# An attention and mixture-of-depths kernel: 1/rms rows stored ahead of the k and v loads, broadcast half a section later, six warm-up products, and tasks moved

## The chip, the cores and the metric

The kernel runs on one core of a Trainium2 chip. Its time is the device time of one execution in microseconds; lower is better. The core's engines are TensorE (PE, the matmuls), VectorE (DVE), ScalarE (ACT), GpSimd (POOL) and SyncE (SP); 16 DMA engines move data between memory and the core. Each engine executes its own list of instructions strictly in order and waits at an instruction until what it depends on is done. SP does no arithmetic here: it issues almost all of the DMAs, in the order of its list.

## What is computed

Per batch of 8: attention of 12 heads over 448 tokens with head size 64, q and k divided by their root mean square, and then a mixture of depths on the 768-wide result: the 128 tokens of each batch with the highest gate score go through a two-layer network.

```python
# q, k, v: (8, 12, 448, 64)
rms = np.sqrt(np.mean(x * x, axis=-1, keepdims=True) + 1e-06)   # of q and of k
q_n, k_n = q / rms_q * g_q, k / rms_k * g_k
scores = q_n @ k_n.T / sqrt(64)
attn = softmax(scores)
x = attn @ v                                  # -> (8, 448, 768)
score = x @ w_gate                            # (8, 448)
top = 128 tokens with the highest score, per batch
out = x.copy()
out[top] = x[top] + sigmoid(score[top]) * (relu(x[top] @ w1) @ w2)   # w1: 768 x 1024
```

Everything is float32.

## The kernel before, in words

**Groups and sections.** Four heads of one batch are a group n, so there are 24 groups. A group has 7 units of 64 keys; for each unit `scores` multiplies k by q (L395), ACT takes the exponential (L404), `values` multiplies by v (L419), and `add_probs` sums the exponentials over the units on DVE (L435). The main loop goes through sections q = 0 to 23, one per group. In section q PE does the scores and values of group q, and between them the finishing work of group q - 1: `sum_keys` (L462, the sums over keys), `invert_sums` (L485, L487) and two transposes back to tokens, `to_tokens` (L517 on PE, L519 on DVE, which evacuates). The first 8 sections (`FIRST = 8`) are halved in two places, A = 0.5 and END = 0.9; later ones have the places MID = 0.4, P0 = 0.6, P1 = 0.75 and P2 = 0.9. From section 9 on, pieces of the network (`mixture`, L720 to L814) are put in at the last three places, `step(q, place)`, except where `SKIP` names the place.

**The planner.** Everything else (loads, normalization, gates, ranks, weights) is a list of tasks with due times in sections, made by `at(time, function)` and carried out by `run(upto)` at the places, in the order of the times and, for equal times, in the order in which they were put on the list. Carrying a task out only writes its instructions at the end of each engine's list. A due time therefore fixes the order on SP, DVE, POOL and ACT, not a time.

**Normalization of q in group n.** `squares` (ACT, L290) and `sum_squares` (DVE L322, then POOL L323, a power of -0.5) give `rinv`, two tiles per group: one for q, one for k. Part k is used by the exponential as its scale. Part q has to be laid along the other axis and is sent through memory: `rows_out` (L334) stores 7 KB to a row, and `rows_in` (L345) loads it, broadcast over 64 partitions, as two DMAs of 224 KB, into `bc`. Then `scale_q` (DVE, L354) multiplies the loaded q by it. Group n's scores in section n need that. `rows_in` can only be issued when the row has landed, and SP waits at it. While FIRST lasts, the times in `prepare` are: store and broadcast both at n - 2 + 0.5, put on the list behind the loads of kT and v of the same group, which have the same time; `scale_q` at n - 1 + 0.5.

**Other names in the change.** `ARRAY[n]` is how many of the 7 units of a group are added by PE in `sum_keys` (8 products more for each) rather than by DVE in `add_probs`. `OTHER_BANK` lists sections whose second `to_tokens` writes into a bank of the scores' PSUM pool (four banks) rather than the one auxiliary bank that `sum_keys` and `invert_sums` use. `MIXED` holds the times at which DVE makes sums of weight blocks (L284) that SP then stores; `PREPARED`, `GATES` and `RANKS` hold exceptions to the times of normalization, of gate products (L545) and of counting, selecting and loading the selected tokens (L591, L618, L641). Weight blocks are loaded by `load_block` (L259).

**The start.** `_build` first computes whether the scores are small enough for the fast variant, and branches. Ahead of the branch PE does 12 products of a zeroed tile (L1569), while `Loads` starts the first loads; behind it `fast` makes an identity on POOL and PE transposes it 9 times (L191). No engine goes past the branch before PE does: the trace shows DVE, ACT and POOL resuming after the last of the 12. The first group's q is scaled without the way through memory, `scale_q_early` (L365, L374).

Of the kernel before, what the change touches and what calls it, by code (L numbers as in the profile page):

```python
# [10 lines left out]
F32 = mybir.dt.float32  # L11
# [6 lines left out]
def _bcast_row(ap_1d: bass.AP, parts: int) -> bass.AP:  # L18
# [1 line left out]

ARRAY = (0, 0, 1, 2, 2, 1, 2, 2, 1, 0, 0, 2, 1, 0, 0, 0, 0, 0, 0, 0, 0, 0, 0, 0)
GATE_PE = {1}
OTHER_BANK = (12, 14, 15, 21)
SKIP = ((8, 0), (8, 1), (8, 2), (11, 2), (13, 2), (14, 1), (17, 2), (18, 2), (19, 0), (19, 2),
 (21, 1), (22, 1), (23, 1), (23, 2))
MIXED = ((1, 1, 0, 8.9), (1, 1, 1, 9.3), (1, 2, 0, 9.6), (1, 2, 1, 10.3), (1, 3, 0, 10.3),
 (1, 3, 1, 10.3), (1, 0, 0, 10.9), (1, 0, 1, 11.4), (2, 1, 0, 11.9), (2, 1, 1, 11.9),
 (2, 2, 0, 12.3), (2, 2, 1, 12.6), (2, 3, 0, 12.6), (2, 3, 1, 13.9), (2, 0, 0, 13.9),  # L30
 (2, 0, 1, 14.6))
PREPARED = {5: {'sq1': 3.5, 'sum0': 2.92},
 6: {'scale': 5.5},
 7: {'out': 5.5},
 8: {'sum1': 6.9},
 10: {'in': 8.92},
 11: {'sum1': 9.75},
 13: {'scale': 12.59},
 14: {'scale': 13.4},
 15: {'out': 13.75},  # L40
 17: {'in': 15.75},
 18: {'in': 16.92, 'out': 16.61},
 20: {'out': 18.89, 'scale': 19.42},
 22: {'out': 20.59},
 23: {'sq0': 20.76}}
GATES = {11: (12.9, 13.3),
 13: (15.3, 15.4),
 17: (18.75, 18.9),
 19: (20.9, 21.3),
 22: (24.4, 24.4)}  # L50
RANKS = {3: (13.6, 13.6, 13.6, 14.4),
 5: (19.75, 19.9, 19.9, 20.3),
 6: (22.75, 23.4, 23.4, 23.9)}


MAX_SCORE = 60.0
# [2 lines left out]
class Loads:  # L59


    def __init__(self, nc, pool, qT, kT, vp, tok, g2):
        self.nc, self.pool = nc, pool
        self.src = {"tok": tok, "qT": qT, "kT": kT, "v": vp}
        self.tiles = {}
        self.groups = tok.shape[1]
        self.gcol = pool.tile([128, 2], F32, name="gcol", bufs=1)
        self.load("tok", 0, 0)
        nc.scalar.dma_start(out=self.gcol, in_=g2)
        neg_half = pool.tile([128, 1], F32, name="neg_half", bufs=1)  # L70
        nc.vector.memset(neg_half, -0.5)

        warm = pool.tile([128, 2], F32, name="warm", bufs=1)
        nc.vector.memset(warm, 1.0)
        nc.scalar.activation(out=warm[:, 0:1], in_=warm[:, 1:2], func=AF.Sqrt)
        self.neg_half, self.warm = neg_half, warm
        self.load("tok", 0, 1)
        self.load("qT", 0)

    def load(self, name, n, i=None):  # L80
        b, g = divmod(n, self.groups)
        src = self.src[name]
        if i is not None:
            src = src[b, g, :, i]
        elif name == "v":
            src = src[b, g]
        else:
            src = src[b, 2 * g : 2 * g + 2].rearrange("c p s -> p c s")
        pool = self.v_pool if name == "v" else self.pool
        bufs = {"tok": 6, "qT": 4, "kT": 3, "v": 3}[name]  # L90
        held = [key for key in self.tiles if key[0] == name]
        if len(held) == bufs:
            del self.tiles[held[0]]
        t = pool.tile(list(src.shape), F32, name=name, bufs=bufs)
# [12 lines left out]
def fast(  # L107
# [21 lines left out]
    nc = tc.nc  # L129

    B, NP, _, S = loads.src["qT"].shape
# [15 lines left out]
    scale = 1.0 / math.sqrt(D)  # L147
# [25 lines left out]
    load, get, neg_half = loads.load, loads.get, loads.neg_half  # L173

    ident = const.tile([128, 128], F32, name="ident")
# [11 lines left out]
    gg = const.tile([128, 1], F32, name="gg")  # L187
    pick_pair = const.tile([128, NJ // 2, 32], F32, name="pick_pair")
    ps = ps_moe.tile([128, 512], F32, tag="moe", name="warm_ps")
    for _ in range(9):  # L190
        nc.tensor.transpose(out=ps[:, 0:128], in_=ident, identity=ident)  # L191

    if len(GATE_PE) < B:
        wg = const.tile([CP, DM], F32, name="wg")
# [253 lines left out]
    def by_array(n):  # L448

        return ARRAY[n]  # L450

# [411 lines left out]
    def at(slot, fn, *args):  # L863
        todo.setdefault(slot, []).append(lambda: fn(*args))
# [8 lines left out]
    A, END = 0.5, 0.9  # L873
    MID, P0, P1, P2 = 0.4, 0.6, 0.75, 0.9

    def prepare(n):
# [12 lines left out]
        if n == 2:  # L889
            times.update(sq0=A, sum0=A, sq1=END, sum1=END, out=A, scale=1 + A)  # L890
            times["in"] = A
        for k, t in PREPARED.get(n, {}).items():
            times[k] = t
# [7 lines left out]
    for n in range(1, n_groups):  # L901
        if n > 2:
            for i in range(2):
                at(n - 5 + P2 if n > 5 else (n - 3) * 0.6, load, "tok", n, i)
        if n > 1:
            at(max(n - 3 + 0.1, 0.3), load, "qT", n)
            at(max(n - 2 + A, 0.3), load, "kT", n)
            at(max(n - 2 + A, 0.3), load, "v", n)
            prepare(n)
    for k, (l, b) in enumerate([(1, b) for b in kept + ((0, 1),)] + [(2, b) for b in kept]):  # L910
        for part in range(2):
            at(2.3 + 0.43 * (2 * k + part), load_block, l, b, part)
    for l, i, part, t in MIXED:
        at(t, mix, l, i, part)
        at(t + 0.25, store_mixed, l, i, part)
# [6 lines left out]
    def after_tokens(n):  # L922
# [11 lines left out]
        else:  # L934
            t = [q + P2, q + 1 + MID]
        t = GATES.get(n, t)
        at(t[0], gate, n, (0, 1))
# [4 lines left out]
    def ranks_of(b):  # L942
# [9 lines left out]
        else:  # L952
            times = [q + P2, q + 1 + MID, q + 1 + MID, q + 1 + P2]
            if b not in GATE_PE:
                times = [q + P0, q + P1, q + P1, q + 1 + 0.3]
        times = RANKS.get(b, times)
        at(times[0], count, b, (0, 1))
# [22 lines left out]
    def add_late():  # L980
# [7 lines left out]
        out=gg, in0=loads.gcol[:, 0:1], scalar=scale, in1=loads.gcol[:, 1:2], op0=OP.mult, op1=OP.mult  # L988
# [28 lines left out]
    def step(q, place):  # L1017
        if (q, place) not in SKIP:
            next(moe)

    waiting = list(range(units))
    for q in range(n_groups):
        u0 = NI * q
        now[:] = q, 0
        b, g = divmod(q, NG)
# [50 lines left out]
        slot[0] = q + P2  # L1076
        to_tokens(q - 1, 1, ps_sc if q in OTHER_BANK else ps_aux)
        if g == 0 and b - 1 in GATE_PE:
# [4 lines left out]
    n = n_groups - 1  # L1083
# [471 lines left out]
def _build(nc, ap, cap, out):  # L1555
    D = ap["g_q"].shape[0]
    with tile.TileContext(nc) as tc, ExitStack() as ctx:
        load_pool = ctx.enter_context(tc.tile_pool(name="load", bufs=1))
        with (
            tc.tile_pool(name="bound", bufs=1) as pool,  # L1560
            tc.tile_pool(name="bound_ps", bufs=1, space=bass.MemoryType.PSUM) as psum,
        ):
            g = pool.tile([1, 2, D], F32, name="g")
            nc.sync.dma_start(out=g, in_=ap["g_row"])
            zeros = pool.tile([128, 128], F32, name="zeros")
            nc.gpsimd.memset(zeros, 0.0)
            ps = psum.tile([128, 128], F32, name="warm_ps")
            for _ in range(12):
                nc.tensor.matmul(out=ps, lhsT=zeros, rhs=zeros, start=True, stop=True)  # L1569
            loads = Loads(nc, load_pool, *(ap[n] for n in ("qT", "kT", "vp", "tok", "g2")))  # L1570


            prod = pool.tile([1, D], F32, name="prod")
            nc.vector.tensor_mul(out=prod, in0=g[:, 0], in1=g[:, 1])
            nc.vector.tensor_mul(out=prod, in0=prod, in1=prod)
            top = pool.tile([1, 1], F32, name="top")
            nc.vector.tensor_reduce(out=top, in_=prod, axis=AX.X, op=OP.max)
            small = pool.tile([1, 1], I32, name="small")
            nc.vector.tensor_scalar(
                out=small,  # L1580
                in0=top,
                scalar1=MAX_SCORE * MAX_SCORE / D,
                scalar2=None,
                op0=OP.is_le,
            )
            is_small = nc.values_load(small[0:1, 0:1], min_val=0, max_val=1,
                skip_runtime_bounds_check_because="a comparison gives 0 or 1")
        with tc.If(is_small > 0) as cmp, tc.manual_schedule():
            fast(
                tc, loads, *(ap[n] for n in _INS[5:]), cap, out,  # L1590
            )
        with cmp.Else():
            general(tc, *(ap[n] for n in _INS), cap, out)
# [47 lines left out]
```

## Time and profile before

| | |
|---|---|
| runs | 512.37, 512.58, 515.81 us; median 512.58 |
| the profiled execution | 514.74 us, of which the span is 513.0 |
| mean granted PE clock | 0.988 of full |
| DVE, ACT, POOL busy | 373.3 (73%), 284.8 (56%), 192.5 us (38%) of the span |
| DMA | 118.44 MB, 231 GB/s on the mean |
| SP waiting at L345 for the stored rows | 126.6 us, 22 times, longest 8.2 |
| row store, from issue to landing | 5.5 to 9.2 us, median 7.3 (22 of them) |
| broadcast, from issue to landing | 3.3 to 5.5 us, median 3.9 (44 DMAs) |

Times in the profile are microseconds from the span's start. "Busy" of PE counts instructions, from first to last, also where the clock is halved. A line such as L354 is the line of the kernel above. "a <-b" in brackets says how long the engine had been idle before the instruction and what ended that. A DMA's line on SP is its issue, not its transfer.

### The profile page before, as it was taken

What the parts mean: (1) busy time and instruction counts of PE and PEld (TensorE: products, weight loads), DVE (VectorE), ACT (ScalarE), POOL (GpSimd) and SP (SyncE); (2) the same over time, 40 slices, a digit from 0 to 9 for tenths busy, and PEclk for the clock granted to TensorE, in tenths of its full rate; (3) what the DMA queues carried; (4) which work ended last, traced back from release to release, by engine and by line L of the source; (5) the groups of instructions that cost most, each with busy time, mean ns of one, the idle gap of its engine ahead of it and who ended that gap; (6) DMA issues with size and microseconds to landing.
All of it is one profiled execution on the core that took longest, in us unless ns stands there. A gap on an engine that the chain in (4) does not pass through costs nothing.

```text
span 513.0 us, 11721 instructions
## 1 busy us (share of the span) xinstructions
PE 482.0 (94%) x4689; PEld 292.9 (57%) x4689; DVE 373.3 (73%) x648; ACT 284.8 (56%) x523; POOL 192.5 (38%) x105
## 2 busy tenths in 40 slices
PE   7999798988879999999999999999999999999992
PEld 6554343444445684654554885754455587858951
DVE  3677687927796999499988888589978876743141
ACT  4878677676757557645567666648635744202200
POOL 0587322654372248040785046043445002031003
PEclk8999999999989999999999999999999999999997
DMA  8777879767987884978587895687547803774621
GB/s 292 230 228 228 271 252 297 241 231 266 316 290 268 271 296 146 310 264 269 180 301 239 279 322 179 234 276 255 162 140 260 270 9 124 244 238 181 209 102 66
DMA packets 55361, 118.44 MB, mean 231 GB/s; under 512 B 12963, under 2 KB 27556, under 8 KB 55298
## 3 DMA queue, kind: packets, MB, share of 16 engines
q1 hardware_dynamic: 51666, 110.66, 64.9%
q0 software_dynamic: 3344, 6.71, 3.8%
q8 instruction: 39, 0.64, 0.5%
q10 hardware_dynamic: 288, 0.23, 0.2%
q14 instruction: 24, 0.20, 0.1%
HBM read 93.81 MB, written 31.64 MB: 245 GB/s over the span
## 4 chain that ended last, share of the span: by engine, by line
PE 51%; DVE 2%; DMA 1%; POOL 1%; issue 1%; POOLq 0%; DVEq 0%
PE sc L395 12%; PE av L419 12%; PE moe_ps L814 7%; PE moe_ps L744 6%; PE side_ps L814 6%; PE side_ps L744 4%; PE x_ps L517 2%; PE den_ps L462 1%; PE xeT_ps L720 1%; DMA out_dram<-xe,row 1%; POOL out_dram L674 1%; PE row_ps L575 1%; DVE prod L545 0%; DVE ring L284 0%; PE den_ps L485 0%
## 5 line engine op out<-in xcount | busy, mean ns | idle before, releaser
L404 ACT ACTIVATE p<-sc,rinv 128x448 f32<-128x448 f32 x336 | 187.6, 641 | 100.2 <-PE sc L395 65.5
L323 POOL TENSOR_TENSOR rinv<-ss,neg_half 128x14 f32<-128x14 f32 x46 | 130.1, 2842 | 158.6 <-DVE ss L322 125.4
L395 PE MATMUL sc<-qT,kT 64*64 64x448 f32 x1344 | 155.5, 547 | 9.8 <-issue 6.9
L419 PE MATMUL av<-p,v 64*64 64x448 f32 x1344 | 149.4, 537 | 0.0
L435 DVE TENSOR_TENSOR sum<-sum,p 128x896 f32<-128x896 f32 x106 | 115.9, 1094 | 4.8 <-ACT p L404 0.2
L395 PEld LDWEIGHTS sc<-qT,kT 64*64 64x64 f32 x1344 | 57.1, 134 | 75.7 <-issue 51.3
L419 PEld LDWEIGHTS av<-p,v 64*64 64x64 f32 x1344 | 62.0, 134 | 64.9 <-issue 57.7
L618 POOL DMA_INDIRECT selected<-x,rank x32 | 41.9, 1309 | 94.9 <-DVE x L610 87.6
L290 ACT ACTIVATE sq<-tok 128x896 f32<-128x896 f32 (+1 forms) x49 | 45.0, 938 | 11.8 <-DVE ss L322 7.4
L322 DVE TENSOR_REDUCE ss<-sq 128x14 f32<-128x910 f32 x46 | 48.6, 1093 | 3.6 <-ACT sq L290 3.6
L519 DVE TENSOR_TENSOR x<-x_ps,rden 112x512 f32<-112x512 f32 x48 | 32.7, 688 | 17.8 <-PE x_ps L517 15.9
L354 DVE SCALAR_TENSOR_TENSOR qT<-qT,gg,bc 128x896 f32<-128x896 f32 x22 | 25.3, 1149 | 24.6 <-DMA bc<-rows 24.6
L545 DVE SCALAR_TENSOR_TENSOR prod<-x,wg 112x448 f32<-112x448 f32 (+1 forms) x56 | 31.2, 557 | 1.4
L517 PE MATMUL x_ps<-ident,xT 128*112 128x128 f32 x192 | 28.9, 276 | 3.1 <-DVE rden L487 3.1
L435 DVE TENSOR_TENSOR sum<-p 128x896 f32<-128x896 f32 x24 | 26.1, 1086 | 1.9 <-ACT p L404 1.8
L674 POOL DMA_INDIRECT out_dram<-xe,row x7 | 7.8, 1120 | 50.7 <-DVE xe L686 44.9
L517 PEld LDWEIGHTS x_ps<-ident,xT 128*112 128x112 f32 x192 | 21.5, 133 | 8.1 <-DVE rden L487 4.8
L442 ACT COPY xT<-av 128x448 f32<-128x448 f32 x48 | 23.3, 539 | 3.3 <-PE av L419 2.9
L814 PE MATMUL moe_ps<-ring,xeT 128*128 128x384 f32 x64 | 22.2, 490 | 1.5 <-DVE xeT L696 1.5
L744 PE MATMUL moe_ps<-xeT,ring 128*128 128x128 f32 x192 | 23.1, 277 | 0.2 <-DVE hT L761 0.2
L591 DVE SCALAR_TENSOR_TENSOR cmp<-score_rows,gate,earlier 112x448 f32<-112x448 f32 x32 | 21.9, 683 | 1.7 <-ACT score_rows L581 1.0
L744 PE MATMUL side_ps<-xeT,w 128*128 128x128 f32 x192 | 22.9, 276 | 0.0
(109 smaller groups left out, 450.1 us busy)
## 6 DMA issues: line engine op xcount, KB each, us to landing
tok<-in_tok_dram SPq DMA_DIRECT2D x47, 448.0 KB, 5.9
ring<-mixed SPq DMA_DIRECT2D x48, 384.0 KB, 4.3
qT<-in_qT_dram SPq DMA_DIRECT2D x24, 448.0 KB, 5.0
kT<-in_kT_dram SPq DMA_DIRECT2D x24, 448.0 KB, 6.9
v<-in_vp_dram SPq DMA_DIRECT2D x24, 448.0 KB, 7.5
out_dram<-x SPq DMA_DIRECT2D x8, 1344.0 KB, 7.8
bc<-rows SPq DMA_DIRECT2D x44, 224.0 KB, 3.9
mixed<-ring SPq DMA_DIRECT2D x16, 384.0 KB, 6.9
```

What stands on the lines that cost most here:

```text
L290: nc.scalar.activation(out=sq[:, h, :, 0:D], in_=t[:, h], func=AF.Square, scale=scale)
L322: nc.vector.tensor_reduce(out=ss, in_=sq, axis=AX.X, op=OP.add)
L323: nc.gpsimd.tensor_tensor(out=rinv.rearrange(flat), in0=ss.rearrange(flat), in1=neg_half.to_broadcast([128, 2 * NI]), op=OP.pow,)
L395: nc.tensor.matmul(out=scs[hh][D * c : D * (c + 1), 0:S], lhsT=get("kT", n)[r, c, D * i : D * (i + 1)], rhs=get("qT", n)[r, c, :], start=True,
L404: nc.scalar.activation(out=p[:, hh], in_=scs[hh][:, 0:S], func=AF.Exp, scale=rinvs[n, 1][:, hh, i : i + 1],)
L419: nc.tensor.matmul(out=avs[n][c][D * hh : D * (hh + 1), 0:S], lhsT=get("v", n)[r, hh, i, :], rhs=probs[u][r, hh], start=(i == 0), stop=(i ...
L435: nc.vector.tensor_tensor(out=sums[n], in0=probs.pop(u - 1) if begins else sums[n], in1=probs.pop(u), op=OP.add)
L517: nc.tensor.transpose(out=ps[:CP, j, :], in_=t[:, j, :], identity=ident)
L519: nc.vector.tensor_tensor(out=xs[b][:, :, col : col + 128].rearrange("p j (h d) -> p j h d", d=D), in0=ps[:CP].rearrange("p j (h d) -> p j ...
L618: w = nc.gpsimd.indirect_dma_start(out=t[:, :], out_offset=bass.IndirectOffsetOnAxis(ap=rank[:, j : j + 1], axis=0), in_=x[:, j, :], in_of ...
L744: nc.tensor.matmul(out=ps[:, 128 * f : 128 * f + n], lhsT=w[:, d, 128 * f : 128 * (f + 1)], rhs=h[:, d, :n], start=first and f == d == 0, ...
L814: nc.tensor.matmul(out=ps[:n, c0:c1], lhsT=h[:, f, :n], rhs=w[:, f, c0:c1], start=first and f == 0, stop=(f == HF - 1), skip_group_check=True,
```

## The change

The list below is the whole of it; entries that merely repeat the default time are left out of the prose but stand in the diff.

- `rows_out` of groups 3 to 7 and 9 is due at n - 2 + 0.3, and of group 10 at 8.3: ahead of kT and v of the same group, and for groups 4 and later behind qT of the next but one. `rows_in` of groups 4 to 9 is due at n - 2 + 0.9, of group 10 at 8.9. Groups 3 and 8 have only one of the two.
- 6 products ahead of the branch, not 12, of a broadcast tile of ones that DVE writes; behind it 8 products of that tile in place of 9 transposes of the identity.
- `ARRAY` is 3 for group 4 (2 before) and 2 for group 5 (1 before).
- `OTHER_BANK` has sections 8, 17 and 20 besides.
- Three weight blocks, three loads, eight block sums, the gate products of group 10, the first sum of group 14, and the ranks of batches 5 and 6 have other times; two pieces of the network move by a section or less (`SKIP`).

```diff
-ARRAY = (0, 0, 1, 2, 2, 1, 2, 2, 1, 0, 0, 2, 1, 0, 0, 0, 0, 0, 0, 0, 0, 0, 0, 0)
+ARRAY = (0, 0, 1, 2, 3, 2, 2, 2, 1, 0, 0, 2, 1, 0, 0, 0, 0, 0, 0, 0, 0, 0, 0, 0)
-OTHER_BANK = (12, 14, 15, 21)
-SKIP = ((8, 0), (8, 1), (8, 2), (11, 2), (13, 2), (14, 1), (17, 2), (18, 2), (19, 0), (19, 2),
+OTHER_BANK = (8, 12, 14, 15, 17, 20, 21)
+SKIP = ((8, 0), (8, 1), (8, 2), (11, 2), (13, 2), (14, 1), (16, 2), (18, 2), (19, 2), (20, 1),
...
-MIXED = ((1, 1, 0, 8.9), (1, 1, 1, 9.3), (1, 2, 0, 9.6), (1, 2, 1, 10.3), (1, 3, 0, 10.3),
- (1, 3, 1, 10.3), (1, 0, 0, 10.9), (1, 0, 1, 11.4), (2, 1, 0, 11.9), (2, 1, 1, 11.9),
- (2, 2, 0, 12.3), (2, 2, 1, 12.6), (2, 3, 0, 12.6), (2, 3, 1, 13.9), (2, 0, 0, 13.9),
+MIXED = ((1, 1, 0, 8.9), (1, 1, 1, 8.9), (1, 2, 0, 9.9), (1, 2, 1, 10.3), (1, 3, 0, 10.3),
+ (1, 3, 1, 10.3), (1, 0, 0, 10.9), (1, 0, 1, 11.6), (2, 1, 0, 11.9), (2, 1, 1, 11.9),
+ (2, 2, 0, 12.6), (2, 2, 1, 12.6), (2, 3, 0, 12.75), (2, 3, 1, 14.3), (2, 0, 0, 14.3),
...
-PREPARED = {5: {'sq1': 3.5, 'sum0': 2.92},
- 6: {'scale': 5.5},
- 7: {'out': 5.5},
- 8: {'sum1': 6.9},
- 10: {'in': 8.92},
+BLOCKS = (2.3, 2.73, 3.16, 3.59, 4.02, 4.45, 4.88, 5.31, 4.74, 6.17, 6.6, 8.03, 7.46, 8.14)
+LOADS = {('kT', 21): 19.3, ('tok', 15): 10.7, ('v', 18): 16.91}
+PREPARED = {3: {'out': 1.3},
+ 4: {'in': 2.9, 'out': 2.3},
+ 5: {'in': 3.9, 'out': 3.3, 'sq1': 3.5, 'sum0': 2.92, 'sum1': 3.89},
+ 6: {'in': 4.9, 'out': 4.3, 'scale': 5.5},
+ 7: {'in': 5.9, 'out': 5.3},
+ 8: {'in': 6.9, 'sum1': 6.89},
+ 9: {'in': 7.9, 'out': 7.3},
+ 10: {'in': 8.9, 'out': 8.3},
...
- 14: {'scale': 13.4},
+ 14: {'scale': 13.4, 'sum0': 11.62},
...
+GATES = {7: (8.9, 9.4),
+ 8: (9.9, 10.4),
+ 10: (11.75, 12.6),
...
+ 20: (21.9, 22.4),
...
-RANKS = {3: (13.6, 13.6, 13.6, 14.4),
- 5: (19.75, 19.9, 19.9, 20.3),
- 6: (22.75, 23.4, 23.4, 23.9)}
+RANKS = {3: (13.6, 13.6, 13.6, 14.4), 5: (19.6, 20.4, 20.4, 20.9), 6: (22.9, 23.4, 23.4, 23.6)}
...
+    def keep_busy(self, ps, times):
+
+        ones = self.warm[:, 1:2].to_broadcast([128, 128])
+        for _ in range(times):
+            self.nc.tensor.matmul(out=ps, lhsT=ones, rhs=ones, start=True, stop=True)
...
-    for _ in range(9):
-        nc.tensor.transpose(out=ps[:, 0:128], in_=ident, identity=ident)
+    loads.keep_busy(ps[:, 0:128], 8)
...
-            at(2.3 + 0.43 * (2 * k + part), load_block, l, b, part)
+            at(BLOCKS[2 * k + part], load_block, l, b, part)
...
-            zeros = pool.tile([128, 128], F32, name="zeros")
-            nc.gpsimd.memset(zeros, 0.0)
-            ps = psum.tile([128, 128], F32, name="warm_ps")
-            for _ in range(12):
-                nc.tensor.matmul(out=ps, lhsT=zeros, rhs=zeros, start=True, stop=True)
             loads = Loads(nc, load_pool, *(ap[n] for n in ("qT", "kT", "vp", "tok", "g2")))
+            loads.keep_busy(psum.tile([128, 128], F32, name="warm_ps"), 6)
```

The loads of tok, qT, kT and v take their times from `LOADS` where it names them; that edit is not shown. Block times of the layer-2 blocks change in three entries: 5.74 to 4.74, 7.03 to 8.03 and 7.89 to 8.14.

More of the change, by code (lines that the diff above doesn't have):

```diff
@@ L45 @@
  23: {'sq0': 20.76}}
-GATES = {11: (12.9, 13.3),
+GATES = {7: (8.9, 9.4),
+ 8: (9.9, 10.4),
+ 10: (11.75, 12.6),
+ 11: (12.9, 13.3),
  13: (15.3, 15.4),
@@ L903, in fast @@
             for i in range(2):
-                at(n - 5 + P2 if n > 5 else (n - 3) * 0.6, load, "tok", n, i)
+                at(LOADS.get(("tok", n), n - 5 + P2 if n > 5 else (n - 3) * 0.6), load, "tok", n, i)
         if n > 1:
-            at(max(n - 3 + 0.1, 0.3), load, "qT", n)
-            at(max(n - 2 + A, 0.3), load, "kT", n)
-            at(max(n - 2 + A, 0.3), load, "v", n)
+            at(LOADS.get(("qT", n), max(n - 3 + 0.1, 0.3)), load, "qT", n)
+            at(LOADS.get(("kT", n), max(n - 2 + A, 0.3)), load, "kT", n)
+            at(LOADS.get(("v", n), max(n - 2 + A, 0.3)), load, "v", n)
             prepare(n)
```

## The prediction

> **What bounds the kernel now.** I read the busy times first, then the chain of waits, then busy time stretch by stretch with the cuts at section starts.
>
> ```profile
> PE 482.0 (94%) x4689; PEld 292.9 (57%) x4689; DVE 373.3 (73%) x648; ACT 284.8 (56%) x523; POOL 192.5 (38%) x105
> ...
> L354 DVE SCALAR_TENSOR_TENSOR qT<-qT,gg,bc 128x896 f32<-128x896 f32 x22 | 25.3, 1149 | 24.6 <-DMA bc<-rows 24.6
> ```
>
> And SP's own waits (what waited for what: us in all, times, longest):
>
> ```profile
> SPq L345 <- DMA rows<-rinv: 126.6, 22, 8.2
> ```
>
> PE is busy 94%, so 31.0 us of idle PE is what scheduling can win, plus whatever a halved clock costs. The chain holds nothing but PE from 231.59 (but for about 5 us at 439 to 444) to 500.5, so that stretch is fixed. The stretches say where the idle time lies (columns: us, then busy PE, PEld, DVE, ACT and POOL with counts, granted clock, DMA share, GB/s):
>
> ```profile
> 0.00:13.16 13.16, 9.38 (x89) 8.79 (x89) 4.97 (x19) 5.29 (x9) 0.89 (x7) 0.87 0.85 294
> ...
> 39.71:55.05 15.34, 13.14 (x139) 5.83 (x138) 9.66 (x12) 11.32 (x20) 8.92 (x6) 1.00 0.76 247
> 55.05:69.02 13.97, 13.09 (x153) 6.22 (x153) 11.48 (x13) 9.81 (x19) 5.12 (x2) 1.00 0.79 259
> 69.02:85.13 16.11, 14.35 (x191) 7.00 (x190) 12.15 (x29) 10.51 (x19) 5.12 (x2) 1.00 0.82 270
> ...
> 98.98:117.18 18.20, 14.63 (x171) 6.55 (x170) 8.26 (x12) 11.27 (x20) 10.48 (x4) 1.00 0.77 262
> 117.18:132.83 15.65, 13.86 (x174) 7.13 (x174) 9.33 (x15) 11.11 (x21) 6.61 (x2) 1.00 0.76 263
> 132.83:149.51 16.68, 14.10 (x174) 8.40 (x174) 15.93 (x28) 10.66 (x19) 10.88 (x6) 1.00 0.87 290
> ```
>
> Sections 2, 3, 4, 6, 7 and 8 leave PE idle 2.2, 0.9, 1.8, 3.6, 1.8 and 2.6 us, 12.9 together; sections 1 and 5 none. The timelines of SP and DVE say why, for group 7:
>
> ```profile
> 104.40 0.38 SPq L334 DMA_DIRECT2D rows<-rinv  x1
> ...
> 111.35 1.11 SPq L345 DMA_DIRECT2D bc<-rows  x2
> ...
> 115.92 1.15 DVE L354 SCALAR_TENSOR_TENSOR qT<-qT,gg,bc 128x896 f32<-128x896 f32 x1 [5.64 <-DMA bc<-rows]
> ...
> 117.18 1.73 PE L395 MATMUL sc<-qT,kT 64*64 64x448 f32 x16 [3.26 <-issue]
> ```
>
> Store, 7 us to landing, broadcast, 4.5 us, scaling, scores: nothing slack. During the store SP issues nothing. In slices of 2 us the DMA moves 407 GB/s at 102 to 104, but 4 GB/s at 110 to 112; likewise 7 at 48 to 50 and 2 at 90 to 92. So the queue runs full behind the loads, empties, and waits for a 7 KB store.
>
> **What the Trainium skill says.** "DMA: Bandwidth & Descriptors", section on two DMAs through the same engine: a dependent DMA must wait for the first one's semaphore, so SP's wait at L345 can't be dropped, only met later. The trace shows it: 126.6 us. "Perfetto Trace Analysis", section "DMA Instruction — HWDGE": the closing semaphore write can be surprisingly late when the target is HBM; the trace agrees, the row lands about 2.5 us after the loads ahead of it have drained (46.7 to 49.2). "TensorE: Matmul & The Clock Gate", Part 1: PE runs at half clock after about 3.4 us of little work and needs as long to recover. The trace agrees twice: clock 0.50 at 10 to 12 us and at 150 to 152. "Perfetto Trace Analysis", "Matmuls", advises rotating groups through PSUM banks; in section 8 a transpose waits 2.29 us for L487, which reads the same auxiliary bank.
>
> **The change, part by part.** (-) is a gain.
>
> *Start.* 12 products take 5.32 us, so 6 take 2.7 and end at 3.7, not 6.37; ones are ready at 0.96, as the zeros were. ACT, DVE and POOL then wait for the first tok halves, issued at 0.79 and 1.21 and landing in 2.7 and 2.8, so ACT starts at about 4.0 rather than 6.53: -2.5. kT, needed next, is done when 1.8 MB have come, which the DMA's slices of 1 us put at about 8.3, before the scores. The spread products L365 take 2.89 us at half clock at 9.5; the same work takes 1.62 (54 of the 56 records) at full clock at 24.7. Eight products are 16 records, 1.8 to 3.5 us at 0.11 to 0.22, which bridge the gap to the spread: -1.2 if the clock holds. I take half: -0.6. Together -3.1; ends: 0 (spread late and cold, first scores cold) and -3.9.
>
> *Rows ahead, broadcast later.* For group 3 SP issues qT at 38.45, two tok (after waiting for PE), kT, v, rows at 40.99. Moved, the row is issued at about 39.9 with 1.34 MB ahead, not 2.24; at 390 GB/s that is 2.3 us, and 1.1 of earlier issue overlaps it. Landing goes from 49.28 to about 46, broadcast from 53.7 to about 50. DVE is free at 49.5, PE needs q at 53.1: the idle 2.2 goes, and the 0.9 of section 3 with it, which is DVE catching up. Its bc stays at 1.5, straight behind v, which hides part of the wait only.
> For group 5 (section 4) broadcast lands at 81.1 and DVE is free at 79.2. Moved, the row has 0.8 MB ahead and lands near 72.5, not 75.9, and the broadcast near 78: most of 1.8 goes, say -1.5.
> For group 7 the row waits for POOL: SP sat 2.4 us until L323 ended at 104.4, behind four L618 and a first L323. Now ring, kT and v stand behind that wait. They go out at 104 rather than 99 to 101.4, land by about 110, and are needed at 114. The row, with nothing ahead, lands near 106.5, the broadcast near 111: the idle 3.6 falls to about 0.8, -2.8, and -0.5 of the 0.8 that L395 lost at 102.5 waiting for k's rinv.
> Group 8's row stays behind v; but SP is no longer held at 111.35 for group 7, so its loads go 4 us earlier. -1.6 of 1.8.
> In section 8 nothing waits for bc, but DVE is busy 15.93 of 16.68 because 4.56 us of waiting pushed its counting (L591) back. That goes, and bank 8 lifts the 2.29. -2.2 of 2.6, and 1.5 of half clock behind it (L395 3.27 for 16 records, else 1.74), of which -1.0. Group 10's scaling waited 3.66; PE lost 1.0 in sections 9 and 10: -0.5.
> Sum -13.2; ends: -3 (row still behind older loads) and -17. A loss is the last rival.
>
> *ARRAY.* 8 products are 16 records, 0.4 us on PE: +0.8 for two. DVE is spared two L435 of 1.09 us, in the sections that feed POOL's late L323; counted above. Bounds 0 to +1.
>
> *Moved tasks.* The block loads, sums, gates, ranks and two network pieces change places among 94% busy PE, not number. SP's queue is passed by three block loads of about 0.4 MB, 1 us each at 390 GB/s, with a full section to their use; kT of 21 and tok of 15 go a place earlier, v of 18 about half a section later, still a section before use. The later rank of batch 5 also moves four L618 on POOL (1.31 each) and the load L641 on SP; it is used in section 21. Its 0.5 section of slack is the cover; without it PE waits about 5 us (landing of L641 4.7). DVE sums of 0.95 are covered by DVE's 83% from 300 to 400. L284 ring sums still pair up ahead of L696 in section 12, so its 1.49 idle stays. Extra score banks could hold the next scores for one L519, 0.69. I take 0; bounds -1.5 and +3.
>
> Sum: -3.1 - 13.2 + 0.8 = -15.5. Each section's end was read against the old order, and as sections shorten DVE, at 21.66 of 22.34 us in section 10, yields less: I take +1.5 for that. -14.0. The profiled execution, 514.74 (513.0 of span), would become 500.7; it stands 2.2 above the median of 512.58, from which I forecast 498.6, rounded to 499.
>
> **The rivals.**
> 1. *DVE or DMA becomes the bound.* Sections 8 to 10 hold 55.1 us of DVE in 60.6; the DMA works at up to 0.88. Then what 2 to 7 win is partly a longer wait in 8 to 10: half of the 13.2 remains. Against: DVE idles 9.9 and 6.3 us in sections 6 and 7, and the DMA stands still 2 to 4 us per section. 512.6 - 3.1 - 6.6 + 0.8 = 504.
> 2. *It doesn't do what it says.* The row's landing is set by older loads and by POOL, and PE still waits. Only the start gains, and a little: 512.6 - 3 = 509.5. Against: 0.9 MB really leave the path.
> 3. *Slower: SP blocked in front of k and v.* The row waits for L323 in SP's list with kT and v behind it. v of 7 went out at 101.4, lands in 7.5, and is used after 117: 8 us of slack. If POOL is later than that in each of groups 4 to 9, PE waits for the excess. To end above 517.7 it must eat 14 and add 5, so about 3 us each over six sections, rinv 11 us late: 519. Against: SP waited for L323 4.7 us in all, 2.4 at most.
>
> **How the numbers follow.** Forecast 0.69, rival 1 0.18, rival 2 0.08, rival 3 0.05. The forecast's own ends are 493 (nearly all idle PE gone, full clock at the start) and 505. The range, 492 to 508.5, takes in rival 1 and leaves out rivals 2 and 3. A difference within 1% (507.5 to 517.7) is what one can't tell from no change: rival 2 and a tail of rival 1, 0.11; slower 0.05; faster 0.84.
>
> **What would show it.** Right: L354 waits for bc under 8 us in all (24.6 now); SP's wait at L345 falls well below 126.6; the first L395 begins at 9 to 10.7 rather than 13.16; section 8 ends by about 137; no DMA slice of 2 us below 20 GB/s between 40 and 140; the stretch from section 13 to the end unchanged within 1 us. Wrong: L395 waiting for kT, L419 for v, or SP over 15 us at L334 for L323; the clock at 0.50 through the spread; idle PE before L744 or L720 in sections 16 to 21.

## The result, and the profile after

The changed kernel takes 507.83 us (median of 17 runs, 503.69 to 512.96), the kernel before, beside it, 513.33 (17 runs, 509.33 to 515.88): a ratio of 0.989, interval 0.9861 to 0.9918. The gain is real, about 5.6 us on 512.58, and less than half of the 14 forecast. The profiled execution took 506.35 us, of which the span is 504.6.

From the page of the changed kernel (L366 is L354 of before), busy time and the costliest groups:

```profile
PE 480.1 (95%) x4716; PEld 295.9 (59%) x4716; DVE 371.3 (74%) x646; ACT 285.3 (57%) x523; POOL 190.7 (38%) x104
...
L366 DVE SCALAR_TENSOR_TENSOR qT<-qT,gg,bc 128x896 f32<-128x896 f32 x22 | 25.2, 1148 | 17.2 <-DMA bc<-rows 14.4
```

And SP's own waits in it:

```profile
SPq L357 <- DMA rows<-rinv: 92.1, 20, 7.4
```

SP waits for the stored rows 34.5 us less than before, yet DVE still waits 14.4 us for the broadcast, where 24.6 should have become less than 8. The stretches cut at section starts (2 to 8, columns as before) show where:

```profile
36.03:49.77 13.74, 12.72 (x139) 5.47 (x138) 11.18 (x13) 10.59 (x20) 8.54 (x6) 1.00 0.83 270
49.77:65.77 16.00, 13.08 (x154) 5.87 (x154) 8.23 (x11) 11.29 (x20) 5.12 (x2) 1.00 0.97 269
65.77:81.64 15.87, 15.87 (x190) 8.05 (x190) 13.78 (x30) 9.88 (x18) 5.41 (x2) 0.89 0.69 215
81.64:99.78 18.14, 14.32 (x203) 7.22 (x202) 10.90 (x24) 11.86 (x22) 10.41 (x6) 1.00 0.99 314
99.78:115.26 15.48, 15.48 (x186) 7.71 (x186) 11.05 (x14) 9.90 (x19) 5.12 (x2) 0.89 0.80 223
115.26:129.04 13.78, 13.78 (x174) 6.73 (x173) 7.61 (x13) 11.14 (x22) 5.13 (x2) 1.00 0.81 257
129.04:144.70 15.66, 13.79 (x174) 6.79 (x173) 14.87 (x27) 11.26 (x20) 10.89 (x6) 1.00 0.94 304
```

Sections 2, 6, 7 and 8 are shorter than before. Sections 3 and 5, where PE lost 0.9 us and nothing, now lose 2.9 and 3.8, and the sections behind them run at a granted clock of 0.89: their busy 15.87 and 15.48 hold 1.7 us each that is only slowness (a version below, mid, does the same work in 14.17 and 13.78). The timeline around the first of these losses, SP, DVE and PE (start, duration, what, idle time before it):

```profile
49.40 0.46 SPq L271 DMA_DIRECT2D w<-in_moe_w_dram  x1
...
49.90 0.47 SPq L112 DMA_DIRECT2D kT<-in_kT_dram  x1
...
50.42 0.47 SPq L112 DMA_DIRECT2D v<-in_vp_dram  x1
...
50.92 0.43 SPq L271 DMA_DIRECT2D w<-in_moe_w_dram  x1
...
53.16 1.10 SPq L357 DMA_DIRECT2D bc<-rows  x2
...
64.52 1.15 DVE L366 SCALAR_TENSOR_TENSOR qT<-qT,gg,bc 128x896 f32<-128x896 f32 x1 [5.30 <-DMA bc<-rows]
...
65.77 2.35 PE L407 MATMUL sc<-qT,kT 64*64 64x448 f32 x16 [2.92 <-issue]
```

SP gets to the broadcast of group 4 early, at 53.16, but straight behind w, kT, v and w, and it lands 11.4 us later. Before, it left into queues that had run empty, and took 3.9 at the median, 5.5 at most. The Trainium skill ("DMA: Bandwidth & Descriptors", "Queues, rings and completion order") says that each DMA engine takes the descriptors of a ring in order; the trace agrees: w, kT, v and w landed at 57.0, 59.5, 61.2 and 62.2, the broadcast behind them by 64.5. The place in the queue is not the whole delay: from 52 to 64 us the DMA engines were 0.85 to 1.10 busy by the trace and yet moved only 166 to 340 GB/s, where the full slices of before reached about 400. Why they were slower there is open. Group 6 repeats it behind more transfers, a 1344 KB store among them:

```profile
82.45 0.69 SPq L545 DMA_DIRECT2D out_dram<-x  x1
...
85.70 2.24 SPq L357 DMA_DIRECT2D bc<-rows  x2
...
98.52 1.15 DVE L366 SCALAR_TENSOR_TENSOR qT<-qT,gg,bc 128x896 f32<-128x896 f32 x1 [6.20 <-DMA bc<-rows]
...
99.78 2.22 PE L407 MATMUL sc<-qT,kT 64*64 64x448 f32 x16 [3.82 <-issue]
```

The account, in us of the two profiled spans, with the version "mid" of the last experiment in the last column (differences against before):

| stretch | forecast | changed kernel | mid |
|---|---|---|---|
| to the first scores | -3.1 | 13.16 to 9.49: -3.7 | -2.7 |
| sections 0 and 1 | 0 | 0.0 | 0.0 |
| sections 2 to 8 | -11.9 | 109.80 to 108.67: -1.1 | 102.84: -7.0 |
| sections 9 to 12 | +1.0 | 84.86 to 81.27: -3.6 | 81.26: -3.6 |
| section 13 to the end | 0 | 278.63 both: 0.0 | -0.1 |
| sum | -14.0 | -8.4 | -13.4 |

(-11.9 is -12.7 for the rows in sections 2 to 8, and +0.8 for ARRAY; +1.0 is -0.5 and the 1.5 given back.) So what is missing was to come from sections 2 to 8, in the step "Rows ahead, broadcast later": 10.8 us, of which the other stretches make up 5.2. The parts are less sure than their sum: a second pair of profiles, described below, gives -1.0, 0.0, -3.7, -3.4 and -0.2 in the same rows, again -8.4 in all. (Each pair shows 8.4 us, repeated runs 5.6: the 17 times of each kernel are spread over some 6 to 9 us.)

### The profile page after: what moved, and what is told of

It is laid out like the page before. It is cut to its first block, busy times and chain, and to the rows that moved or that the text cites. A ratio compares the mean times of both kernels' runs of the same rounds, so it can differ in the third digit from the quotient of the medians.

```text
span 504.6 us, 11762 instructions
## 1 busy us (share of the span) xinstructions
PE 480.1 (95%) x4716; PEld 295.9 (59%) x4716; DVE 371.3 (74%) x646; ACT 285.3 (57%) x523; POOL 190.7 (38%) x104
## 2 busy tenths in 40 slices
DMA packets 55361, 118.44 MB, mean 235 GB/s; under 512 B 12963, under 2 KB 27556, under 8 KB 55298
## 4 chain that ended last, share of the span: by engine, by line
PE 73%; DMA 4%; DVE 2%; issue 1%; POOL 1%; SPq 0%; ACT 0%; POOLq 0%; DVEq 0%
PE sc L407 18%; PE av L431 18%; PE moe_ps L756 9%; PE moe_ps L826 8%; PE side_ps L826 6%; PE side_ps L756 6%; PE x_ps L529 3%; PE den_ps L474 2%; DMA bc<-rows 2%; PE xeT_ps L732 1%; DMA rows<-rinv 1%; DMA out_dram<-xe,row 1%; PE row_ps L587 1%; POOL out_dram L686 1%; DVE prod L557 0%
## 5 line engine op out<-in xcount | busy, mean ns | idle before, releaser
L335 POOL TENSOR_TENSOR rinv<-ss,neg_half 128x14 f32<-128x14 f32 x46 | 130.1, 2841 | 159.4 <-DVE ss L334 137.7
L431 PE MATMUL av<-p,v 64*64 64x448 f32 x1344 | 152.4, 544 | 0.0
L447 DVE TENSOR_TENSOR sum<-sum,p 128x896 f32<-128x896 f32 x104 | 113.7, 1093 | 5.3 <-ACT p L416 0.9
L407 PEld LDWEIGHTS sc<-qT,kT 64*64 64x64 f32 x1344 | 58.5, 133 | 74.6 <-issue 47.4
L431 PEld LDWEIGHTS av<-p,v 64*64 64x64 f32 x1344 | 64.8, 135 | 63.8 <-issue 55.6
L630 POOL DMA_INDIRECT selected<-x,rank x32 | 40.0, 1250 | 89.1 <-DVE x L622 81.6
L334 DVE TENSOR_REDUCE ss<-sq 128x14 f32<-128x910 f32 x46 | 48.7, 1092 | 3.6 <-ACT sq L302 3.6
L366 DVE SCALAR_TENSOR_TENSOR qT<-qT,gg,bc 128x896 f32<-128x896 f32 x22 | 25.2, 1148 | 17.2 <-DMA bc<-rows 14.4
L756 PEld LDWEIGHTS moe_ps<-xeT,ring 128*128 128x128 f32 x192 | 22.1, 192 | 1.0 <-issue 0.5
```

Of the source, the lines that this page charges most:

```text
L334: nc.vector.tensor_reduce(out=ss, in_=sq, axis=AX.X, op=OP.add)
L335: nc.gpsimd.tensor_tensor(out=rinv.rearrange(flat), in0=ss.rearrange(flat), in1=neg_half.to_broadcast([128, 2 * NI]), op=OP.pow,)
L407: nc.tensor.matmul(out=scs[hh][D * c : D * (c + 1), 0:S], lhsT=get("kT", n)[r, c, D * i : D * (i + 1)], rhs=get("qT", n)[r, c, :], start=True,
L431: nc.tensor.matmul(out=avs[n][c][D * hh : D * (hh + 1), 0:S], lhsT=get("v", n)[r, hh, i, :], rhs=probs[u][r, hh], start=(i == 0), stop=(i ...
L447: nc.vector.tensor_tensor(out=sums[n], in0=probs.pop(u - 1) if begins else sums[n], in1=probs.pop(u), op=OP.add)
L630: w = nc.gpsimd.indirect_dma_start(out=t[:, :], out_offset=bass.IndirectOffsetOnAxis(ap=rank[:, j : j + 1], axis=0), in_=x[:, j, :], in_of ...
```

## The experiments

Theory after this reading: the broadcasts of groups 4 and 6 queue behind loads. Rivals: the bytes themselves (the DMA's share in sections 3 to 8 was 0.69 to 0.99), SP held in front of the loads, or losses that fall where they happen to.

**One part alone, groups 4 and 6 put back, and everything ahead of qT's load.** start_only is the kernel before with the new warm-up products; rows_only is the kernel before with the times of `out` and `in` of groups 3 to 10. The other two change the changed kernel:

```diff
 g46_back
- 4: {'in': 2.9, 'out': 2.3},
- 6: {'in': 4.9, 'out': 4.3, 'scale': 5.5},
+ 6: {'scale': 5.5},
 all_ahead (n = 3 to 9)
+ n: {'out': n - 2 + 0.05, 'in': n - 2 + 0.06}
```

> The kernel before with the edit of the start alone (6 and 8 products of ones for 12 and 9). Theory (each edit's gain is where the traces put it): the first scores L395 begin near 9.5 us, not 13.2, and nothing later takes it back, so 3.7 us less: about 509.5 if before is at 513.3, ratio 0.993. Rival (the DMA is full and takes back what PE wins): the first scores begin at 9.5, but section 3 begins less than 2 us earlier than before and the ratio is above 0.997.

Measured: 510.78 us, ratio 0.9931 (0.9893 to 0.9968). That is 3.5 us (interval 1.6 to 5.5), so the start alone is worth about what was forecast for it.

> The kernel before with the times of the row store and the broadcast of groups 3 to 10 alone. Theory (the broadcast of groups 4 and 6 is now issued behind loads that are still in the DMA rings): L354 of groups 4 and 6 waits for bc 4 us or more each, with about 10 us from issue to landing, while groups 3, 7 and 8 together wait under 5 (14.5 before); the two effects about cancel, 509 to 514 us. Rival (POOL or DVE were late, not the DMA): the waits of groups 4 and 6 are not there without the change of ARRAY and of the blocks, and the time is below 507.

Measured: 513.69, ratio 0.9994 (0.9962 to 1.0026). The time is the one expected, the waits are not: group 4 waited 2.38 us only, group 6 4.35, and groups 3, 7 and 8 waited 7.8 together and not under 5. The rows alone, as placed here, gain nothing that repeated runs show.

> The changed kernel with the row store and broadcast of groups 4 and 6 at their old times. Theory: the waits of 5.3 and 6.2 us at L366 for groups 4 and 6 fall below 2 us each, the half clock after them goes, and 6 to 9 us are won against the changed kernel: 499 to 502 (ratio to before 0.973 to 0.978). Rival (the DMA is full whatever the order): waits for bc come back at other groups, and the time stays within 2.5 us of the changed kernel's 507.8.

Measured: 506.18, ratio 0.9852 (0.9806 to 0.9898). A miss for the theory, and the time is what the rival said: group 6 waited no longer, yet section 5 took 19.05 us, and groups 4, 5 and 7 waited 2.81, 2.55 and 2.63.

> The changed kernel with row store and broadcast of groups 3 to 9 both ahead of the load of qT that waits for PE anyway (due n - 2 + 0.05 and 0.06). Theory: each broadcast meets a nearly empty ring and lands in 3 to 5 us, L366 waits for bc under 4 us in all, only group 7 (whose row waits for POOL) may hold loads up; 497 to 501. Rival (full DMA): the loads behind come later by what the broadcast comes earlier, PE waits for kT or v, and the time stays at 505 to 508.

Measured: 506.37, ratio 0.9837 (0.9784 to 0.9891). The waits for bc of groups 3 to 6 are gone, those of 7 and 8 are 0.62 and 0.68, and the time is about the same. SP's waits between 40 and 145 us tell one reason:

```profile
SPq L357 <- DMA rows<-rinv: 47.6, 6, 9.5
```

In the changed kernel that stretch held 16.0. With the wait for the rows ahead of qT, kT and v, SP issues none of them during it; in slices of 2 us the DMA falls to 4 to 16 GB/s at 52, 82, 104 and 118. A second reason is section 5, 21.15 us long, of which more below.

**Do the losses repeat?** Both kernels profiled once more, unchanged.

> The kernel before, profiled once more, to see what repeats. If stalls are set by the order of the queues: span 512 to 515, section 5 about 13.9 us long with no trickling of the den_ps products, and the wait of the scale for the broadcast within 1 us of 2.77, 4.27, 0.52, 1.89, 0, 5.64, 4.56, 0, 3.66 us in groups 2 to 10. If stalls fall where they happen to: one of the sections differs by over 3 us.

Measured: 514.29 us, span 512.6. Section 5 took 15.56 rather than 13.85, the start was 1.4 shorter, and the other sections were within about 0.6 of the first profile. Neither expectation came: no section differs by 3 us, but the waits for the broadcast did not repeat within 1 us (group 8 waited 1.38 and not 4.56, group 4 1.99 and not 0.52).

> The changed kernel, profiled once more. If the two new waits are set by where the broadcasts of groups 4 and 6 stand in SP's queue: 4.5 to 6 us of waiting for bc in each of them again, half clock after both, section 3 about 16 us and section 5 about 18 us, span 503 to 507. If they happened by chance: at least one of them under 2 us.

Measured: 505.89 us, span 504.2. The wait of group 4 was 3.90 (5.30 in the first profile), of group 6 2.12 (6.20), and section 5 lost 7.2 us in another way, for which see the next runs. The expectation of two fixed waits failed: the end differs by 0.4 us only, but the losses in between lie elsewhere.

**What happens in section 5.** In all_ahead, start_only, g46_back and after_again PE stumbles in the products `den_ps` (the sums over keys, in one burst) there: it goes on in handfuls. These two runs move work that stands beside them; both are all_ahead with

```diff
+RANKS = {0: (4.9, 4.9, 5.5, 5.9), 3: ...
-            at(s, store_x, b)
+            at(s + 0.95 if b == 0 else s, store_x, b)   # second run only
```

> The version with store and broadcast both ahead of qT's load, and the select of batch 0 (four scatter DMAs from POOL) half a section later. Theory that the scatters, beside the transfers of section 5, starve the burst of den_ps products: section 5 falls from 21 us to at most 15, ratio at most 0.975, profiled execution about 499. Rival, that the loads and the store alone do it: section 5 stays over 18 us and the ratio at 0.981 to 0.987. Second rival, that it happens by chance: section 5 short here and the ratio all the same at 0.981 to 0.987.

> As the run ahead of it, and the store of batch 0's output 1344 KB moved behind the burst of den_ps products too. Theory of the scatters: no more than 1 us from the run ahead of it. Theory that the store is what fills the queues in the burst: this one alone has a section 5 of at most 15 us, ratio at most 0.975, and the one ahead of it stays at 0.984. By chance: neither differs from 0.984 by over 0.005.

Measured: 506.63, ratio 0.9846 (0.9805 to 0.9886), and 506.87, 0.9851 (0.9803 to 0.99). Section 5 fell to 15.27 and 14.86 us, with no stumbling, but the gain was gone one section later. A short section 5 and the ratio all the same is what the second rival named; it called that chance, but the traces show a cause. In ahead_sel, on PE's timeline:

```profile
114.89 3.27 PE L407 MATMUL sc<-qT,kT 64*64 64x448 f32 x16 [5.96 <-DMA kT<-in_kT_dram]
```

SP had waited 11.1 us for the rows, from 94.4 to 105.6, and kT's load, behind that in its list, left at 107.86. In ahead_both PE waited 4.21 us for kT at the same place. This is the loss that rival 3 described, SP blocked in front of the loads, but it is the landing of the row that blocks it and not POOL.

**Are the bytes the limit?** Each kernel without the stores of batches 0 and 1 (`if b > 1` ahead of the task `store_x`), and each with half token tiles in groups 3 to 9.

> The changed kernel without the stores of the outputs of batches 0 and 1 (two transfers of 1344 KB, in sections 5 and 8; those two batches' outputs are then incomplete). Transfers as the limit of sections 3 to 8: the first store stood in the queues ahead of the broadcast of group 6, so that wait falls from 4.4 to 6.2 us to under 2.5, section 9 starts at 140 to 142 us and not at 144, ratio 0.977 to 0.982 (502 to 504). Rival, the order of waits on SP and not the bytes: section 9 at 143.5 to 145, ratio 0.987 to 0.991.

Measured: 505.61, ratio 0.9825 (0.9777 to 0.9872); section 9 began at 144.63. Group 6 no longer waited, as the theory had it, but section 5 stumbled and took 19.02 us.

> The same two stores left out of the kernel before. Its queues pause behind the rows anyway, so the bytes are worth less: section 9 starts within 1.5 us of 149.3, ratio 0.996 to 1.000. If transfers bound the kernel before just as much: section 9 at 145.5 to 147.5, ratio 0.992 to 0.995.

Measured: 506.44, ratio 0.9865 (0.9822 to 0.9909); section 9 began at 142.36.

> The changed kernel with half of each token tile of groups 3 to 9 loaded, 224 KB and not 448 (14 transfers, 3.1 MB less, about 8 us of all queues; the squares read the loaded half twice, so these groups' norms are made of half the tokens). Transfers as the limit of sections 2 to 7: waits of the scale for the broadcast add up to under 8 us and not 14, section 9 starts at 137 to 140, ratio 0.968 to 0.976 (497 to 501). Rival, the order of waits on SP: section 9 at 143 to 145, ratio 0.986 to 0.991.

Measured: 506.01, ratio 0.9855 (0.9781 to 0.993); section 9 began at 143.50. The waits add up to 10.3 us, and section 5 stumbled (21.02 us).

> The same halves left out of the kernel before. Queues that pause anyway: section 9 within 2 us of 149.3, waits for the broadcast within 3 us of the 24.6 in all, ratio 0.995 to 1.000. If transfers bound the kernel before just as much: section 9 at 142 to 145, ratio 0.984 to 0.989.

Measured: 510.78, ratio 0.9936 (0.991 to 0.9961). Section 9 began at 144.10. For the changed kernel the theory of bytes isn't borne out: with 2.8 or 3.2 MB less it starts section 9 at most 1.2 us earlier (144.70 and 144.26 with all of them), where 2.5 to 7 were expected. Nor is it excluded as a part, since both intervals reach below that of the changed kernel and section 5 stumbled in both profiles. The kernel before, whose bytes were expected to be worth less, gained 6.9 and 3.3 us, so its transfers do count. That the bytes are not what held the changed kernel back is shown better by the version mid below: it moves the same 118.44 MB and is about 7 us faster.

**Is the stumbling a shortage of instructions?** In all_ahead the burst of section 5 stopped 49 records in, and the next packet of the larger queue of instructions (39 packets, 0.64 MB; taken to be PE's, which has most instructions) came after the burst. The shift puts tiny products ahead, 2 records each:

```diff
     scale_q_early(0)
+    loads.few(shift_ps, 30)      # 60 in after_s120
```

> The version with store and broadcast ahead of qT's load, with 30 tiny products (60 records of TensorE, 32 by 8 values, on no result) behind the products that spread the first 1/rms. Theory that the burst of section 5 ran out of instructions at a fixed place in the program: the place moves 60 records forward, out of the burst of 80, the trickle is gone from section 5, which takes at most 15.5 us and not 21.2; the start loses 0 to 1 us; ratio 0.970 to 0.977 (499 to 502) unless another stretch runs dry instead. Rival, that the burst itself or the transfers beside it make the trickle: it is there again, 42 to 49 records into the burst, section 5 over 19 us, ratio 0.983 to 0.987.

> The version with groups 4 and 6 at their old times, with the same 60 records. Instructions: no trickle in section 5, which takes at most 15.5 us and not 19.1, ratio 0.970 to 0.978. Rival: trickle again, ratio 0.984 to 0.988.

> The changed kernel with the same 60 records. Instructions: no trickle in section 5; the waits of groups 4 and 6 for their broadcasts stay at 4 to 6 us each, since they are of another kind, so section 5 at 14 to 18 us and the ratio at 0.980 to 0.989. Rival, burst or transfers: as the second profile of the changed kernel, section 5 at 21 us with the trickle 49 records into the burst, ratio 0.986 to 0.991.

> The changed kernel with 60 tiny products, 120 records, about one whole packet of instructions: the boundaries come back to where they were. Instructions: the burst of section 5 may trickle as in the second profile of the changed kernel, again 40 to 50 records into it, or it waits for the broadcast as in the first one; the ratio is 0.988 to 0.994, with 1 to 2 us lost at the start. Rival, that extra records ahead help by themselves: the same as the version with 60.

Measured: 504.84, 507.64, 505.6 and 507.95 us; ratios 0.9853 (0.977 to 0.9935), 0.9891 (0.9863 to 0.9918), 0.9843 (0.9761 to 0.9926), 0.9894 (0.9793 to 0.9995). The trickle was in none of the four, and section 5 of all_ahead_s60 took 14.25 us (80.62 to 94.87), but no time moved beyond its interval: g46_s60 lost 3.77 us ahead of section 7, after_s60 2.62 ahead of section 4 and 4.99 ahead of section 6. By after_s120, where it might have returned and didn't, and by the last run below, the theory isn't confirmed.

**Between store and broadcast, something else to issue.** The changed kernel with other due times of `rows_out` and `rows_in` in groups 3 to 9, and nothing else:

```diff
+ n: {'out': n - 2 + 0.05, 'in': n - 2 + 0.45}     # n = 3 to 9
```

On SP the order becomes rows, qT of the group after it (the traces show qT of n + 1 there, not the next but one that is named further up), a block w for some groups, broadcast, kT, v. mid and all_ahead differ in the due time of the broadcast alone. The second run adds the 60 records.

> The changed kernel with the rows of groups 3 to 9 stored ahead of qT's load and the broadcast behind it, ahead of kT's and v's loads: SP has qT's issue to do while the rows land. If the broadcast's place on SP is what is left of the loss: waits of the scale for the broadcast under 5 us in all in groups 3 to 9, waits of SP for the rows 25 to 40 us (47.6 with both ahead of qT), ratio 0.972 to 0.979 (499 to 502). If each stretch gained there is lost at the next thing that is fetched late (instructions, kT, rows): ratio 0.981 to 0.987, and the profile shows a stall of 3 us or more in a section where 0.984 had none.

> The same with the 60 records. If the trickle of section 5 costs repeated executions as much as the profiled ones (6 to 7 us, less what the start loses): a ratio lower than that of the run ahead of it by 0.006 to 0.012. If a profiled execution is one draw among several losses of like size: within 0.004 of it.

Measured: **501.81 us, ratio 0.9745 (0.9712 to 0.9779)**, and 502.0, 0.9742 (0.9712 to 0.9772). The first theory is met in its time and its waits; the rows hold SP even less than expected. The 60 records change nothing, and both profiles have the trickle, so what it costs repeated executions wasn't found out. SP's waits for the rows in mid between 40 and 145 us:

```profile
SPq L357 <- DMA rows<-rinv: 11.3, 6, 3.8
```

SP does not wait less in all: 64 us in this stretch of mid, 62 in all_ahead, 65 in the changed kernel. It waits elsewhere. In mid 10.8 us are spent at qT's load, for PE to be done with the buffer (1.0 in all_ahead); that wait stands between store and broadcast, so the row lands during it. Another 34.8 are spent at the loads of tok, for ACT (6.1 in all_ahead), when kT and v have been issued. The row then follows fewer loads that are still under way: from its store to the broadcast's issue SP needs 3.1 to 5.3 us in groups 4 to 9, in all_ahead 7.2 to 10.5.

DVE's scaling in mid, for groups 4 and 6 (no idle time in brackets, so no wait):

```profile
59.75 1.15 DVE L366 SCALAR_TENSOR_TENSOR qT<-qT,gg,bc 128x896 f32<-128x896 f32 x1
...
92.84 1.15 DVE L366 SCALAR_TENSOR_TENSOR qT<-qT,gg,bc 128x896 f32<-128x896 f32 x1
```

The same stretches in mid, sections 3 to 6:

```profile
50.38:63.40 13.02, 13.02 (x155) 5.84 (x154) 9.90 (x12) 10.54 (x20) 5.13 (x2) 1.00 0.92 276
63.40:77.57 14.17, 14.17 (x191) 7.02 (x190) 11.62 (x27) 10.49 (x19) 5.41 (x2) 1.00 0.94 290
77.57:97.56 19.99, 17.86 (x203) 8.14 (x202) 13.06 (x26) 11.10 (x22) 10.26 (x6) 0.91 0.88 286
97.56:111.34 13.78, 13.78 (x186) 6.61 (x185) 8.89 (x11) 10.51 (x20) 5.13 (x2) 1.00 0.83 251
```

Sections 3, 4 and 6 have no idle PE and the full clock: 3.0 us less than the changed kernel in section 3, 1.7 each in 4 and 6. Of these only section 5 loses. mid beats both kernels, with an interval that meets neither that of the changed kernel (0.9861 to 0.9918) nor that of all_ahead (0.9784 to 0.9891).

## Why the prediction was right or wrong

**Direction and bound, right.** Idle PE in sections 2 to 8 was there to win: 12.8 us before, 3.7 in mid.

**Start, right in direction, its size in part by luck.** -3.1 forecast, -3.7 in the first pair of profiles, 0.9931 alone (-3.5). The spread began at 7.05 and took 1.68 us at full clock, where it had taken 2.89 at half. But the half clock was not fixed in the kernel before: in its second profile the spread took 1.68 us too, and the pair shows only -1.0. The five profiles with the old start have their first scores at 10.92 to 13.20 (mean 12.0), the ten with the new one and without the 60 records at 9.49 to 10.68 (mean 10.2).

**Rows ahead, broadcast later: the step that failed.** It was to give -13.2, of which -12.7 in sections 2 to 8, and gave -1.1 there in one pair of profiles and -3.7 in the other, with ARRAY's cost included. It went wrong in two ways. It put the landing of a broadcast about 4 us behind its issue, a duration that the trace of before had shown only with queues run empty, and at the same time moved the broadcasts behind kT, v and the weight blocks: 11.4 us. And it costed groups 3, 5, 7, 8 and 10, which had waited before, not 4 and 6, which had waited 0.52 and 0 and were moved as well. Their waits of 5.30 and 6.20, PE's idle 2.92 and 3.82, and 3.4 us of half clock behind them took 10.1 us of the first profiled execution. Putting only these two groups back did not win that (g46_back, 0.9852); placing store and broadcast anew in all of groups 3 to 9 did. That the order on SP's list is the cause is shown by mid: with the broadcast between qT and kT the same term reaches -7.0. The size that was forecast is not shown to be reachable. By an estimate it would be about -12.7 without the 5.7 that section 5 still loses (19.99 against 14.25 in all_ahead_s60), but all_ahead_s60, ahead_sel and ahead_both, whose section 5 is short, lost other sections instead.

**A reading of the row's landing, wrong.** The prediction took the loads ahead of group 3's row to be done at 46.7 and the row's 2.5 us more for a late closing write. The DMA packets of before say otherwise. Up to 48.6 packets of 3.5 KB still followed each other one at a time, then came the row's last ones, of 28 bytes, until 48.7, and SP knew of the landing at 49.3, 0.6 later. So the row had waited for the slowest part of the loads ahead of it. The same holds for the rows of groups 4 to 9, whose last packets come within 0.1 us of the end of the last large one, in the kernel before and in all_ahead.

**ARRAY +0.8 and moved tasks 0.** ARRAY lies in sections 5 and 6, where the sums of groups 4 and 5 are made, and wasn't measured by itself; the 16 records more took 0.39 us in undisturbed bursts of section 5 (1.72 us against 1.33 behind the first 16), as forecast. Sections 9 to 12 gave -3.6 where -0.5 and +1.5 had been forecast; the +1.5 for DVE did not come. Of this 1.4 lie in section 10 (22.34 to 20.93), and they go with the rows: rows_only, which moves no other task, takes 20.92 there, and group 10, which had waited 3.66 us for its broadcast, waits no longer. The 1.8 in section 12 (22.66 to 20.90) go with the other edits: PE no longer waits 1.49 us for L696, a wait that the prediction had let stand and that is 0.4 to 1.5 us long in before, before_again, rows_only and start_only. There the term of the moved tasks was mis-sized. Which of them did it was not tried.

**Rivals.** What came, about 507 on the forecast's scale, lies between rival 1's 504 and rival 2's 509.5. Rival 1's mechanism, DMA or DVE as the bound, isn't borne out as far as bytes go: 3.2 MB less left section 9 of the changed kernel nearly where it was, and mid moves all of them. Rival 2, that the rows stay as late as they were, is near the truth for the rows as placed here (0.9994 alone); the whole gains some 2 us more than the start, which section 12 can account for, though the intervals of 0.9931 and 0.989 overlap. Rival 3 did not occur in the changed kernel (SP waited for L335 9.3 us in all, 4.6 at most), but a relative of it costs all_ahead and ahead_sel their gain: there SP's waits for the row's landing stand in front of kT.

**The signs named.** First scores at 9.49, a shorter wait of SP for the rows and an unchanged end were right, and no slice of 2 us fell below 20 GB/s between 40 and 140 (22 at 76). The wait for bc under 8 us was wrong (14.4), and so was section 8 ending by 137 (144.7).

## What to carry to other kernels

A load that depends on a store, in a queue that one engine issues in order, can be late in two ways: ahead of the big loads it holds the issuer, behind them it waits in the queues. What worked here was to put between store and load an issue that has to wait for something else anyway, so that the store lands meanwhile, and the big loads behind. When a transfer is moved, take its duration from a trace in which the same transfers stand ahead of it, and cost the instances that had no wait too.

## What the runs showed that was not expected

**A burst of PE that trickles beside POOL's scatters.** In eight of the twenty profiles the products `den_ps` of section 5 went on in handfuls, each after about 0.3 us for which the trace names no cause. In mid, PE's timeline:

```profile
84.23 1.02 PE L474 MATMUL den_ps<-p,pick_pair 128*32 128x112 f32 x33
85.44 0.44 PE L474 MATMUL den_ps<-p,pick_pair 128*32 128x112 f32 x7 [0.18 <-issue]
86.20 0.38 PE L474 MATMUL den_ps<-p,pick_pair 128*32 128x112 f32 x3 [0.33 <-issue]
86.91 0.43 PE L474 MATMUL den_ps<-p,pick_pair 128*32 128x112 f32 x5 [0.33 <-issue]
87.67 0.40 PE L483 MATMUL den_ps<-xT,hT 128*32 128x112 f32 x5 [0.33 <-issue]
...
```

and POOL's, in the same kernel:

```profile
84.17 1.16 POOL L630 DMA_INDIRECT selected<-x,rank  x1 [11.76 <-DVE x L622]
...
88.16 0.94 POOL L630 DMA_INDIRECT selected<-x,rank  x1 [0.30 <-issue]
```

The 64 records behind the first 16 take 1.7 us undisturbed and 5.9 here; half clock follows (0.50 at 90 to 92). In all eight the trickle begins 1.1 to 2.4 us after the first of the four scatters of batch 0's selection and ends 1.1 to 1.6 us after the last; it is missing in both runs in which the scatters were moved away, and in the five in which they began when the burst was all but over. PE's last pause ends 0.74 to 0.90 us after the end of the last scatter in all eight, whether 1 or 25 records of the burst are left, and what is left then runs on. But five profiles had burst and scatters at the same moment without it, and in these one scatter took about 2.1 us rather than 0.95. So it looks as if either POOL or PE is held; by what stays open. The Trainium skill ("Runtime: NRT & Kernel Launch", "Instruction fetch mechanics") says that instructions come in blocks of 16 KiB by DMA, mostly hidden. The packets' size agrees (0.64 MB in 39), but a late packet as the cause isn't shown: mid_s60, shifted by 60 records, trickled at nearly the same place of the burst (53 records in, 49 in mid), and a packet landed in the midst of it. mid with the selection moved as well was not tried; by section 5 alone, an estimate is up to 5.7 us more, though in ahead_sel and ahead_both the gain did not last.

**One profile is one draw.** Two profiles of the changed kernel end 0.4 us apart, with section 3 at 16.00 and 14.61 us and section 5 at 18.14 and 21.34.
